# Two attention heads in the partition halves: masked keys, a shorter diagonal and 64-row value products in a four-block kernel

## The chip, the cores and the metric

One core of a Trainium2 chip runs the program. The metric is the device time of one execution in microseconds (us); the kernel before has a median of 531.84 us over three runs (530.72 to 532.0). The engines are named as in the profile: PE (TensorE matmul) with its weight loads PEld, DVE (VectorE), ACT (ScalarE), POOL (GpSimd) and SP (SyncE, which issues most DMAs).

## What is computed

The input is 2048 tokens of 512 features. Four residual blocks follow each other, A, B, A, B, with layer norm ahead of each. Both have 32 heads of 16 features. A is attention in four segments of 512 tokens, causal within the segment, plus a read from a memory that gathers the earlier segments. B is linear attention with softmax feature maps.

```python
# A, for each segment s of 512 tokens (q, k, v: head, token, 16)
logits = einsum('bhqd,bhkd->bhqk', qs, ks) * 0.25 + mask     # mask: -1e9 above the diagonal
a_dot = einsum('bhqk,bhkd->bhqd', softmax(logits), vs)
a_mem = einsum('bhld,bhde->bhle', phi(qs), M) / (einsum('bhld,bhd->bhl', phi(qs), z) + 1e-6)
out_s = g * a_mem + (1 - g) * a_dot                          # g = sigmoid(beta), per head
M += einsum('bhld,bhle->bhde', phi(ks), vs); z += sum_l phi(ks)
# B, over all 2048 tokens
phi_q = concat(softmax(q @ w_phi), softmax(-q @ w_phi))      # phi_k alike
o = phi_q @ (phi_k^T v) / (phi_q @ sum(phi_k) + 1e-6)
```

## The kernel before

The whole input lives in SBUF as 16 token tiles of 128 rows. Each operation is an entry of a graph (`Graph.op`, line 130) with its reads and writes; a table written out in the file (ORDER, line 979) gives the order of all operations, the engine of those that may run on two, and the buffer of each tile. `place` (line 156) reads it, `emit` (line 189) writes one instruction stream per engine with semaphore waits. So each engine takes its work strictly in the table's order, and nothing is rearranged when the program runs.

Block A. `a_proj` (line 610) makes one segment's operands for four groups g of eight heads: keys KT and queries QT (128 features x 512 tokens), and from QT four masked copies Q4 (line 642), each of which keeps every fourth head. Values VT are token-major, 17 columns for a head, the last of them ones, so that a product with them gives the softmax denominator too. `a_att` (line 677) handles one token tile of 128 queries, i being its place in the segment. For each group and each block j <= i of 128 keys:

- a logits product fills a two-bank PSUM buffer S (pool pD, two buffers): two matmuls, one for each 64-row half hf of the features, with 128 keys as weights and four masked query copies (512 columns) moving. The result is 128 keys x 8 heads x 128 queries;
- ACT takes the exponential of 1024 columns into a tile PT of SBUF (line 701 calls the helper at 329);
- on the diagonal, j = i, POOL zeroes what lies above it with two affine selects of 512 columns (line 705);
- PE multiplies: for each head PT's 128 keys x 128 queries are the weights and VT's 17 columns move, written two or three times over by the access pattern of `pvitem` (line 670), so 34 or 51 columns. Sums run over j in a value bank PV of PSUM (pool pG; two such banks).

One bank PV holds two groups (line 688). Behind its two groups come, from segment 1 on, small products for the memory's denominator in the same bank (line 719, eight columns, and an epsilon row), a reciprocal (line 723, helper 367) and a multiply (line 725), both on DVE; meanwhile the other bank takes the next two groups. Then the memory read (line 731), the transpose of the result by a DMA on SP, and the output projection (line 738) with the residual.

Block B. `b_keys` (line 812) and `b_query` (line 848) share the engines: key blocks of B are interleaved with A's later tiles, B's queries follow after the last segment, since they need all keys. All matmuls are issued by the helper at line 323, most exponentials by 329, PSUM copies by 337 (ACT) and 338 (DVE).

A warm-up (line 591) keeps PE running while the first loads land. It holds some matmuls on the 64-row form, pairs in which one works on feature rows 0 to 63 and the other on rows 64 to 127.

Of the kernel before, what the change touches and what calls it, by code (L numbers as in the profile page):

```python
# [9 lines left out]
ACT = mybir.ActivationFunctionType  # L10
# [6 lines left out]
D = 512  # L17
H = 32
# [276 lines left out]
class Kernel:  # L295
# [78 lines left out]
    def alloc(self):  # L374
# [8 lines left out]
        self.eps8 = sb("eps8", [128, 8], BF16)  # L383
# [37 lines left out]
        self.pools = [self.pK, self.pX, self.pQ, self.pV, self.p1, self.p2, self.pT, self.pS, self.pD, self.pG]  # L421
# [5 lines left out]
    def setup(self):  # L427
# [38 lines left out]
        for g in range(NG):  # L466
# [34 lines left out]
        for i, tv in enumerate(self.pV.tensors):  # L501
            self.pV.init[i] = v(lambda e, tv=tv: e.memset(tv[:, :, :, 16:17], 1.0), 560, [], [], eng=P, label="one")
        v(lambda e: e.tensor_copy(self.Rz1[:, :, :, 1], self.H8[:, None, :].to_broadcast([128, 8, 8])), 130,
# [87 lines left out]
    def warm(self):  # L591
# [12 lines left out]
        for k in range(N_WARM):  # L604
            unit(128, 512, 1)
            if k == N_WARM // 2:
                for rows, n, m, c0 in ((64, 51, 12, 0), (64, 17, 8, 64), (64, 51, 8, 0), (64, 128, 8, 0), (128, 34, 8, 0), (128, 34, 8, 64), (128, 34, 8, 0)):
                    unit(rows, n, m, c0)

    def a_proj(self, L, s):  # L610
# [3 lines left out]
        st["KT"], st["Q4"], st["PhQ"], st["PhK"] = [], [], [], []  # L614
        VT = st["VT"] = self.T(self.pV, "VT")
        first = (L, s) in MASKED
        for g in range(NG):
# [3 lines left out]
            KT = self.T(self.pK, "KT")  # L621
# [3 lines left out]
            st["KT"].append(KT)  # L625
# [10 lines left out]
            QT = self.T(self.p1, "QT")  # L636
            Q4 = self.T(self.pQ, "Q4")
# [3 lines left out]
            for sl in range(4):  # L641
                fn = lambda e, Q4=Q4, QT=QT, sl=sl: e.tensor_scalar(Q4.t[:, sl, :], QT.t[:], self.m4[:, sl:sl + 1], None, op0=ALU.mult)  # L642
                self.g.op({"dve": (262.0, fn)}, [QT, R("m4")], [Q4[sl]], label="Qm", port=True)
            st["Q4"].append(Q4)
# [3 lines left out]
        for tt in range(4):  # L648
            ps = self.T(self.pG, "gen")
            self.vproj(ps, self.WA["v"], [R("WAv", i) for i in range(4)], tt, xT, opens=[VT], label="V")  # L650
            self.evac(lambda tt=tt: VT.t[:, tt, :, 0:16], lambda ps=ps: ps.t[:, 0:512].rearrange("p (h d) -> p h d", h=H),
                      512, [ps[0]], [VT[tt]], label="Vev")
        if s < 3:
            for hp in range(2):
                ps = self.T(self.pG, "gen")
                gs = (hp * 2, hp * 2 + 1)
                self.mm(lambda gs=gs, ps=ps: [(ps.t[:, (g % 2) * 136:(g % 2 + 1) * 136], st["PhK"][g].t[:, tt * 128:(tt + 1) * 128],
                                               VT.t[:, tt, 8 * g:8 * g + 8, :], tt == 0, tt == 3) for g in gs for tt in range(4)],
# [10 lines left out]

    def pvitem(self, PV, c, P, V, st, sp):  # L670

        n = 3 if 2 * c >= 2 * PVW - 495 and c >= PVW - 400 and c + 2 * (PVW - c) <= 495 else 2
        a = PV.t[:, c:c + 17]
        w = int(a.ap[0][0])
        return (bass.AP(a.tensor, int(a.offset), [[w, 128], [PVW - c, n], [1, 17]]), P, V[:, None, :].to_broadcast([128, n, 17]), st, sp)

    def a_att(self, L, s, i):
        R, v = self.R, self.v
        st = self.seg[(L, s)]
        VT = st["VT"]  # L680
        t = s * 4 + i
        Rt = self.T(self.pS, "R")
        rden = lambda: Rt.t[:, 0:64].rearrange("p (h k) -> p h k", k=2)
        o = self.T(self.p1, "o")
        nk = 2 if s >= 1 else 1
        mb = s - 1
        for hp in range(2):
            PV = self.T(self.pG, "pv")
            pvv = lambda PV=PV: PV.t[:, 0:288].rearrange("p (h c) -> p h c", c=18)
            for gg in range(2):  # L690
                g = hp * 2 + gg
                KT, Q4 = st["KT"][g], st["Q4"][g]
                PTs = []
                for j in range(i + 1):
                    S = self.T(self.pD, "S")
                    PT = self.T(self.p2, "PT")
                    self.mm(lambda S=S, KT=KT, Q4=Q4, j=j: [
                        (S.t[:, hf * 512:(hf + 1) * 512], KT.t[64 * hf:64 * hf + 64, j * 128:(j + 1) * 128],
                         Q4.t[64 * hf:64 * hf + 64, :, i * 128:(i + 1) * 128], True, True) for hf in range(2)],
                        [512], [KT] + [Q4[sl] for sl in range(4)], [S], opens=[PT], label="S", rows=64)  # L700
                    self.act(lambda PT=PT: PT.t[:], lambda S=S: S.t[:], ACT.Exp, 1024, [S], [PT], scale=0.25, label="exp")
                    if j == i:
                        for hh in range(2):
                            pt4 = lambda PT=PT, hh=hh: PT.t[:, hh * 512:(hh + 1) * 512].rearrange("p (h q) -> p h q", h=4)
                            v(lambda e, pt4=pt4: e.affine_select(pt4(), pt4(), [[0, 4], [1, 128]], ALU.is_ge, 0.0, base=0, channel_multiplier=-1),  # L705
                              587, [PT], [PT[hh]], eng="pool", label="mask")
                    PTs.append(PT)

                def pvmm(PV=PV, PTs=PTs, g=g, gg=gg):
                    r = []  # L710
                    for hl in range(8):
                        c = (gg * 8 + hl) * 18
                        for j in range(i + 1):
                            r.append(self.pvitem(PV, c, PTs[j].t[:, hl * 128:(hl + 1) * 128], VT.t[:, j, 8 * g + hl, :], j == 0, j == i))
                    return r
                self.mm(pvmm, [17] * (8 * (i + 1)), PTs + [PTs[i][0], PTs[i][1]] + [VT[j] for j in range(i + 1)], [PV[gg]], label="PV")
                if s >= 1:
                    PQ = st["PhQ"][g]
                    self.mm(lambda PV=PV, PQ=PQ, g=g, gg=gg, pvv=pvv: [
                        (pvv()[:, gg * 8:gg * 8 + 8, 17], PQ.t[:, i * 128:(i + 1) * 128], self.MSb[mb][:, g, :, 16], True, False),  # L720
                        (pvv()[:, gg * 8:gg * 8 + 8, 17], self.onesb[:], self.eps8[:], False, True)],
                        [8, 8], [PQ, PV[gg], R("MSb", mb, hp), R("onesb"), R("eps8")], [PV[("d", gg)]], label="NMd")
            v(lambda e, pvv=pvv, hp=hp: self.recip(e, rden()[:, hp * 16:hp * 16 + 16, 0:nk], pvv()[:, :, 16:16 + nk]), self.dur_recip(16 * nk),
              [PV[0], PV[1]] + ([PV[("d", 0)], PV[("d", 1)]] if s >= 1 else []), [Rt[hp]], label="rden")
            v(lambda e, pvv=pvv, hp=hp: e.tensor_tensor(o.t[:, hp * 256:(hp + 1) * 256].rearrange("p (h d) -> p h d", h=16), pvv()[:, :, 0:16],  # L725
                                                        rden()[:, hp * 16:hp * 16 + 16, 0:1].to_broadcast([128, 16, 16]), ALU.mult), 340,
              [PV[0], PV[1], Rt[hp]], [o[hp]], label="pvn")
        if s >= 1:
            NM = self.T(self.pG, "nz")
            tmp = self.T(self.p1, "nmt")  # L730
            self.mm(lambda: [(NM.t[:, g * 128:(g + 1) * 128], st["PhQ"][g].t[:, i * 128:(i + 1) * 128], self.MSb[mb][:, g, :, 0:16], True, True)
                             for g in range(NG)], [128] * 4, list(st["PhQ"]) + [R("MSb", mb, 0), R("MSb", mb, 1)], [NM], opens=[tmp], label="NM")
            v(lambda e: e.tensor_tensor(tmp.t[:].rearrange("p (h d) -> p h d", h=H), NM.t[:, :].rearrange("p (h d) -> p h d", h=H),
                                        rden()[:, :, 1:2].to_broadcast([128, H, DH]), ALU.mult), 602, [NM, Rt[0], Rt[1]], [tmp], label="nmn")
# [175 lines left out]
    def build(self):  # L910
# [9 lines left out]
        for L in range(2):  # L920
            if L == 0:
                lnA(0, 0)
                gate = self.xnop[3]
                for o in self.loads[self.early:self.second] + list(self.pV.init.values()):
                    o.deps.add(gate)
# [38 lines left out]
N_XT, N_Q4, N_K1, N_K2, N_VT, N_SM, N_KT = 5, 6, 22, 19, 5, 6, 6  # L964
PVW = 288
CAP1 = {"KT": 8, "QT": 4, "phiQ": 8, "PhK": 4, "E": 8, "xn": 3, "phe": 3, "phiKT": 2}
CAP2 = {"EQ": 16, "ET": 6}
# [12 lines left out]
c-rlEW0)<=vTa6M?e1mUwr$(CZQHhO+qP}nHg8t<+Iz3Han8H<y<hj8n%|r`D>E`MB4T7!G!z996dlDt;ZZ>p6(LjzML-f2Mu3W-qNo_cC?YD3!l6h=p%N  # L980
$wq9`&diAo`cN~2t;3=*g;Du<Gyn24kDr~=B3Dxx$f52}RnqRJ>4iiPr_<fsZti&CJ>NTd8HF-nK3qV&k1*r)(XgtDMbs2Z{;E2@sNp&BRy%8qKHj3_0_f
ij^~C?~3gQlr|a4yubfpcbej>V&$XmZ%HrjJl#$s2^&L;-Ky*E3`rV(HN8f#Y5R3A)1Baqp_$5ii_%@*{D7mgqET4Xdar2mY@M>Ihup+q8zXQEk)VkB3gt
7qlM@ax`)Q02`DEFL=DhlG!ZpKx!^jwjP9dG=nBdWjnQe;1U*1a(GAoLok8<abMz2hMUPNh)DyKsz0gfG1ocMk(KU1n^+9LRZ8Q{3LO!T3I){d#JE$NGN0
ZTcv;vJlg&;3nK*eAsN(*^l6`F#kB41P-Mxttv52hhMR2W8~bl{JwLrN$C`5^#>$3<W?ssX{M0MvyLR1;pIk`Mt$#X%?{j*TPXKvWM1yhgPl71W1lxE5?f
# [109 lines left out]
```

## Time and profile before

| | |
|---|---|
| median of three runs | 531.84 us |
| the profiled execution | 537.12 us, its span 535.1 us |
| mean granted TensorE clock | 0.990 |
| exponentials of 1024 columns | 384, mean 1041 ns (320 of the attention) |
| masks on POOL | 256, busy 164.0 us |
| mask multiplies on DVE (line 642) | 128, mean 389 ns |
| logits matmuls, 64 rows | 640, mean 387 ns |
| value matmuls, 34 or 51 columns | 2560, a mean of 179 or 187 ns |

How to read the profile: the busy time of an engine is the union of its instructions. A matmul's own time includes its way through the array, so matmuls that follow each other closely overlap in the list, and the distance of their starts tells what one of them costs. A line of the groups gives line, engine, operation, out<-in, the shapes with their count, then busy us and mean ns of one, then the idle time ahead of them with what ended it. A line of the waits names who waited for whom, the total in us, how often, and the longest. "issue" stands where nothing that the profile shows was waited for. The form "64*128" of a matmul says that it uses 64 rows and 128 columns of the array.

### The profile page before, as it was taken

To read this page: it belongs to the slowest core of one execution; us is meant where nothing else is said; L and a number is where in the kernel's file an instruction comes from. 1 tells how busy PE (TensorE), PEld (TensorE's weight loads), DVE (VectorE), ACT (ScalarE), POOL (GpSimd) and SP (SyncE) were. 2 spreads that over 40 slices of the span, in tenths; PEclk is the share of its full clock that TensorE was granted. 3 is DMA by queue.
4 is the path that set the end of the run, shared out by engine and by line. 5 is a ranking of instruction groups with operands and counts; after the bars stand their busy time and mean duration, and the time that the engine had idled before them with its cause. 6 is when DMAs were issued, how large, how long until landed. Compare 5 with 4: busy or idle time off the path is not lost.

```text
span 535.1 us, 13744 instructions
## 1 busy us (share of the span) xinstructions
PE 491.3 (92%) x5587; PEld 260.3 (49%) x5664; DVE 459.3 (86%) x1083; ACT 474.7 (89%) x616; POOL 220.9 (41%) x392
## 2 busy tenths in 40 slices
PE   9887799999999999999998879998999999999886
PEld 4333345354555455556643444453544555455653
DVE  5989999997977989778999989986988988867865
ACT  4688999999999989877997999997999999988964
POOL 4468356435645442201350753643184375320000
PEclk9999999999999999998999999998999999999989
DMA  8099332211121110000343241131111211100245
GB/s 236 19 234 137 59 70 32 50 22 30 32 41 22 21 35 17 11 2 1 61 78 70 50 80 27 24 52 22 31 21 31 31 22 31 31 13 1 50 110 137
DMA packets 84990, 27.39 MB, mean 51 GB/s; under 512 B 75680, under 2 KB 84928, under 8 KB 84928
## 3 DMA queue, kind: packets, MB, share of 16 engines
q1 hardware_dynamic: 84864, 26.50, 25.6%
q8 instruction: 44, 0.72, 0.6%
q14 instruction: 18, 0.15, 0.1%
q0 software_dynamic: 64, 0.02, 0.1%
HBM read 6.32 MB, written 2.10 MB: 16 GB/s over the span
## 4 chain that ended last, share of the span: by engine, by line
PE 46%; DVE 28%; ACT 17%; DMA 5%; issue 2%; POOL 1%; SPq 0%
PE G L323 29%; ACT p L329 16%; PE D L323 14%; DVE pQ L642 4%; DMA p<-p 4%; DVE stats L538 3%; DVE p L588 2%; PE D L601 2%; DVE pS L826 2%; DVE p L586 1%; DVE p L587 1%; DVE p L900 1%; DVE X L765 1%; DVE p L338 1%; DVE p L725 1%
## 5 line engine op out<-in xcount | busy, mean ns | idle before, releaser
L329 ACT ACTIVATE p<-D 128x1024 bf16<-128x1024 f32 x384 | 376.1, 1041 | 27.7 <-PE D L323 24.2
L705 POOL TENSOR_SCALAR_AFFINE_SELECT p<-p 128x512 bf16<-128x512 bf16 x256 | 164.0, 665 | 154.4 <-ACT p L329 153.7
L323 PE MATMUL D<-pQ,pK 64*128 64x512 bf16 x640 | 117.5, 387 | 5.6 <-ACT p L329 4.2
L323 PE MATMUL G<-pV,p 128*128 128x51 bf16 (+2 forms) x2656 | 93.5, 186 | 3.4 <-DVE p L725 2.1
L323 PEld LDWEIGHTS G<-pV,p 128*128 128x128 bf16 x2656 | 80.8, 96 | 29.7 <-issue 16.9
L329 ACT ACTIVATE p<-G 128x512 bf16<-128x512 f32 x112 | 67.6, 618 | 5.2 <-PE G L323 3.5
L323 PEld LDWEIGHTS D<-pQ,pK 64*128 64x128 bf16 x640 | 29.5, 93 | 75.2 <-ACT p L329 32.8
L546 POOL TENSOR_SCALAR rstd<-mv 128x1 f32<-128x1 f32 x60 | 17.0, 285 | 99.3 <-DVE mv L539 97.4
L826 DVE TENSOR_REDUCE pS<-p 128x32 f32<-128x512 bf16 x64 | 42.4, 675 | 13.8 <-ACT p L329 13.7
L642 DVE TENSOR_SCALAR pQ<-p,m 128x512 bf16<-128x512 bf16 x128 | 44.1, 389 | 3.5 <-ACT p L337 2.2
L538 DVE BATCH_NORM_STATS2 stats<-X 128x6 f32<-128x512 bf16 x64 | 43.3, 683 | 2.7 <-DMA X<-in_A_x_dram 1.6
L765 DVE TENSOR_TENSOR X<-X,G 128x512 bf16<-128x512 bf16 x48 | 32.4, 676 | 11.8 <-PE G L323 10.8
L808 DVE TENSOR_TENSOR pT<-G,pT 128x1024 bf16<-128x1024 f32 x30 | 36.5, 1215 | 4.8 <-PE G L323 4.3
L548 POOL TENSOR_TENSOR rstd<-rstd,mhalf 128x1 f32<-128x1 f32 x60 | 36.5, 612 | 3.5
L323 PE MATMUL G<-WA_o,p 128*128 128x512 bf16 x117 | 30.6, 380 | 4.6 <-DMA p<-p 2.2
L323 PE MATMUL G<-WB_k,pX 128*128 128x512 bf16 x119 | 31.2, 386 | 3.8 <-DMA pX<-p 2.6
L323 PE MATMUL G<-WB_o,p 128*128 128x512 bf16 x123 | 33.2, 394 | 1.0 <-DMA p<-p 0.4
L323 PE MATMUL G<-WA_v,pX 128*128 128x512 bf16 x120 | 30.5, 380 | 3.4 <-DVE p L725 1.7
L323 PE MATMUL G<-pX,WA_q 128*128 128x512 bf16 x118 | 30.1, 380 | 3.6 <-DVE mv L539 2.0
L323 PE MATMUL G<-WB_v,pX 128*128 128x512 bf16 x115 | 30.7, 382 | 1.8 <-issue 0.7
L323 PE MATMUL G<-pX,WA_k 128*128 128x512 bf16 x118 | 30.3, 380 | 1.2 <-issue 0.8
L323 PE MATMUL D<-pX,WB_q 128*128 128x512 bf16 x120 | 29.6, 379 | 0.5
(103 smaller groups left out, 669.9 us busy)
## 6 DMA issues: line engine op xcount, KB each, us to landing
out_dram<-X SPq DMA_DIRECT2D x16, 128.0 KB, 1.8
X<-in_A_x_dram SPq DMA_DIRECT2D x3, 512.0 KB, 6.2
pX<-in_B_wqkv_dram SPq DMA_DIRECT2D x3, 512.0 KB, 5.3
p<-p SPq DMA_TRANSPOSE x76, 2.5
pX<-p SPq DMA_TRANSPOSE x54, 2.5
X<-in_A_x_dram SPq DMA_DIRECT2D x4, 128.0 KB, 2.2
WA_k<-in_A_wk_dram SPq DMA_DIRECT2D x2, 256.0 KB, 4.8
WA_q<-in_A_wq_dram SPq DMA_DIRECT2D x2, 256.0 KB, 4.9
```

The lines of the kernel that those rows point to most:

```text
L323: ins = e.matmul(out_ap, lhsT, rhs, start=st, stop=sp, tile_position=(basep(lhsT), basep(out_ap)))
L329: return self.g.op({"act": (dur, lambda e: e.activation(out_ap(), in_ap(), func, scale=scale))}, reads, writes, opens, label=label)
L538: v(lambda e: e.bn_stats(self.stats[:, t, :], self.X[:, t, :]), 602, [R("X", t)], [R("st", t)], label="bn")
L546: v(lambda e: e.tensor_scalar(rs, self.mv[:, t, 1:2], LN_EPS, None, op0=ALU.add), 170, [R("mv", t)], [R("rstd", t)], eng="pool", label="rstd")
L548: v(lambda e: e.tensor_tensor(rs, rs, self.mhalf[:], ALU.pow), 540, [R("rstd", t), R("mhalf")], [R("rstd", t)], eng="pool", label="rstd")
L588: v(lambda e: e.tensor_tensor(dst.t[:], dst.t[:], e_.t[:], ALU.add), 335, [dst, e_], [dst], label="phadd", port=True)
L601: ins = e.matmul(D.t[c0:, r0 * 8:r0 * 8 + n], r[:, c0:], ones(r, n), start=True, stop=True, tile_position=(r0, c0))
L642: fn = lambda e, Q4=Q4, QT=QT, sl=sl: e.tensor_scalar(Q4.t[:, sl, :], QT.t[:], self.m4[:, sl:sl + 1], None, op0=ALU.mult)
L705: v(lambda e, pt4=pt4: e.affine_select(pt4(), pt4(), [[0, 4], [1, 128]], ALU.is_ge, 0.0, base=0, channel_multiplier=-1), 587, [PT], [PT[hh ...
L765: self.v(lambda e: e.tensor_tensor(self.X[:, t, :], self.X[:, t, :], ps.t[:, 0:512], ALU.add), 602, [R("X", t), ps[0]], [R("X", t)], label ...
L808: v(lambda e: e.tensor_tensor(dst(), ps.t[:, None, 0:512].to_broadcast([128, 2, 512]).rearrange("p s (g d h) -> p s g d h", g=NG, h=8), rz ...
L826: fn = lambda e, sgn=sgn, E=E, Z=Z: e.tensor_reduce(Z.t[:, sgn * 32:(sgn + 1) * 32], E.t[:, sgn * 512:(sgn + 1) * 512].rearrange("p (h d) ...
```

## The change

The mask moves from the queries to the keys. `a_proj` now makes KM from KT: for each half hf of the features, each of two head pairs p and each half x of a key block, a weight of 64 rows x 128 columns, whose columns 0 to 63 are 64 keys for one head and columns 64 to 127 the same keys for another. The count of multiplies stays at four per group and segment. A logits product then puts one head in partitions 0 to 63 and another in 64 to 127, and takes eight matmuls of 128 moving columns (two halves hf x two pairs x two key halves) in place of two of 512.

On the diagonal the second half of the keys needs only the second half of the queries, so a block has 192 columns for a pair of key halves, 768 in all. The triangle is added by a product: two more matmuls (weights `two64`, moving `tri`, 256 columns) add -1e9 where a query precedes its key. The POOL masks are not issued (PMASK has every tile). The exponentials of a diagonal block go to new tiles (pool pE, four buffers), whose first 64 columns are zeroed once at the start.

The value products take 64 rows each: 16 of them for a group and a key block, alternately on partitions 0 to 63 into one bank and on 64 to 127 into the other. Where the key half does not stand in the right partitions, they read VS, a copy of half of the values with the partition halves swapped, which two DMAs on SP make for each segment. Both value banks stay open over all four groups of a token tile; then each is normalized. The memory's denominators are one product of an epsilon row and four of eight columns for the whole tile, with a reciprocal of their own.

Buffers: p1 22 to 20, p2 19 to 18, the cap of B's exponentials 16 to 12. The warm-up has other shapes. The order table is new as a whole.

```diff
+            KM = self.T(self.pQ, "KM")
+            for sl in range(4):
+                fn = lambda e, KM=KM, KT=KT, sl=sl: e.tensor_scalar(
+                    KM.t[:, :, sl % 2, :, 64 * (sl // 2):64 * (sl // 2) + 64], KT.t[:].rearrange("p (j h k) -> p j h k", j=4, h=2),
+                    self.m4[:, sl:sl + 1], None, op0=ALU.mult)
-            for sl in range(4):
-                fn = lambda e, Q4=Q4, QT=QT, sl=sl: e.tensor_scalar(Q4.t[:, sl, :], QT.t[:], self.m4[:, sl:sl + 1], None, op0=ALU.mult)
...
+        for z in range(VSP):
+            t0, t1 = z * 4 // VSP, (z + 1) * 4 // VSP
+            for hf in range(2):
+                a = lambda hf=hf, t0=t0, t1=t1: VS.t[64 * hf:64 * hf + 64, t0:t1]
+                b = lambda hf=hf, t0=t0, t1=t1: VT.t[64 - 64 * hf:128 - 64 * hf, t0:t1, 16 * hf:16 * hf + 16, :]
+                self.g.op({"sp": (650.0, lambda e, a=a, b=b: [e.dma_start(a(), b())])}, [VT[i] for i in range(t0, t1)], [VS[(z, hf)]],
+                          kind="d", lat=1900.0, label="vsw", ndma=1)
...
-        n = 3 if 2 * c >= 2 * PVW - 495 and c >= PVW - 400 and c + 2 * (PVW - c) <= 495 else 2
-        return (bass.AP(a.tensor, int(a.offset), [[w, 128], [PVW - c, n], [1, 17]]), P, V[:, None, :].to_broadcast([128, n, 17]), st, sp)
+        k = int(V.ap[0][1])
+        return (bass.AP(a.tensor, int(a.offset), [[w, 128], [PVW - c, 2], [1, 17]]), P, V[:, None, :].to_broadcast([k, 2, 17]), st, sp)
...
+                    for p in range(2):
+                        for x in range(2):
+                            for hf in range(2):
+                                c = hf * 512 + (p * 192 + 64 * (1 - x) if dg else p * 256 + x * 128)
+                                c0 = 64 if dg and x else 0
+                                r.append((S.t[:, c:c + 128 - c0], k(hf, p, x), q(hf, c0), not (dg and pem) or p + x == 0, not (dg and pem)))
+                    if dg and pem:
+                        for hf in range(2):
+                            r.append((S.t[:, hf * 512:hf * 512 + 384].rearrange("p (a b) -> p a b", a=2)[:, :, 0:128], self.two64[64 * hf:64 * hf + 64].rearrange("p a b -> p (a b)"),
+                                      self.tri[64 * hf:64 * hf + 64, None, :].to_broadcast([64, 4, 64]), False, True))
...
+                    self.act(lambda PT=PT: PT.t[:, :, 64:256], lambda S=S: S.t[:, :].rearrange("p (a b) -> p a b", a=2)[:, :, 0:384].rearrange("p a (c e) -> p a c e", c=2),
+                             ACT.Exp, 768, [S], [PT], scale=0.25, label="expd")
...
+            def pvmm(PTs=PTs, g=g):
+                r = []
+                for hf in range(2):
+                    for p in range(2):
+                        k = 4 * g + 2 * hf + p
+                        for j in range(i + 1):
+                            for x in range(2):
+                                for ab in range(2):
+                                    if j == i:
+                                        P = PTs[j].t[64 * ab:64 * ab + 64, hf * 2 + p, 128 * (1 - x):128 * (2 - x)]
+                                    else:
+                                        c = hf * 512 + p * 256 + x * 128
+                                        P = PTs[j].t[64 * ab:64 * ab + 64, c:c + 128]
+                                    V = VT.t[64 * ab:64 * ab + 64, j, 16 * ab + k, :] if x == ab else VS.t[64 * ab:64 * ab + 64, j, k, :]
+                                    r.append(self.pvitem(PV[ab], 18 * k, P, V, j == 0 and x == 0, j == i and x == 1))
+                return r
...
+            self.mm(lambda: [(mc(), self.onesb[:], self.eps32[:], True, False)] +
+                    [(PV[0].t[:, 288 + 8 * g:296 + 8 * g], PQ[g].t[:, i * 128:(i + 1) * 128], self.MSb[mb][:, g, :, 16], False, g == NG - 1) for g in range(NG)],
+                    [32] + [8] * 4, list(PQ) + [R("MSb", mb, 0), R("MSb", mb, 1), R("onesb"), R("eps8")], [PV[0]["d"]], label="NMd")
...
-N_XT, N_Q4, N_K1, N_K2, N_VT, N_SM, N_KT = 5, 6, 22, 19, 5, 6, 6
-PVW = 288
+N_XT, N_KM, N_K1, N_K2, N_VT, N_SM, N_QT, N_PE = 5, 6, 20, 18, 5, 6, 6, 4
+PVW = 320
+VSP = 1
+PMASK = {(L, t) for L in range(2) for t in range(16)}
```

More of the change, by code (lines that the diff above doesn't have):

```diff
@@ L502, in setup @@
             self.pV.init[i] = v(lambda e, tv=tv: e.memset(tv[:, :, :, 16:17], 1.0), 560, [], [], eng=P, label="one")
+        for i, tp in enumerate(self.pE.tensors):
+            self.pE.init[i] = v(lambda e, tp=tp: e.memset(tp[:, :, 0:64], 0.0), 330, [], [], eng=P, label="one")
         v(lambda e: e.tensor_copy(self.Rz1[:, :, :, 1], self.H8[:, None, :].to_broadcast([128, 8, 8])), 130,
@@ L606, in warm @@
             if k == N_WARM // 2:
-                for rows, n, m, c0 in ((64, 51, 12, 0), (64, 17, 8, 64), (64, 51, 8, 0), (64, 128, 8, 0), (128, 34, 8, 0), (128, 34, 8, 64), (128, 34, 8, 0)):
-                    unit(rows, n, m, c0)
+                for rows, n, m in ((64, 51, 12), (64, 64, 8), (64, 256, 4), (128, 34, 8)):
+                    unit(rows, n, m)
     def a_proj(self, L, s):
@@ L649, in a_proj @@
             ps = self.T(self.pG, "gen")
-            self.vproj(ps, self.WA["v"], [R("WAv", i) for i in range(4)], tt, xT, opens=[VT], label="V")
+            self.mm(lambda tt=tt, ps=ps: [(ps.t[:, 0:512], xT.t[:, dt, tt * 128:(tt + 1) * 128],
+                                           self.WA["v"][:, dt, :].rearrange("p (k a e) -> p a k e", k=8, a=2), dt == 0, dt == 3) for dt in range(4)],
+                    [512] * 4, [xT[tt]] + [R("WAv", i) for i in range(4)], [ps[0]], opens=[VT], label="V")
             self.evac(lambda tt=tt: VT.t[:, tt, :, 0:16], lambda ps=ps: ps.t[:, 0:512].rearrange("p (h d) -> p h d", h=H),
                       512, [ps[0]], [VT[tt]], label="Vev")
+        for z in range(VSP):
[5 more added lines that the diff above has]
+                          kind="d", lat=1900.0, label="vsw", ndma=1)
         if s < 3:
@@ L656, in a_proj @@
                 gs = (hp * 2, hp * 2 + 1)
-                self.mm(lambda gs=gs, ps=ps: [(ps.t[:, (g % 2) * 136:(g % 2 + 1) * 136], st["PhK"][g].t[:, tt * 128:(tt + 1) * 128],
-                                               VT.t[:, tt, 8 * g:8 * g + 8, :], tt == 0, tt == 3) for g in gs for tt in range(4)],
+                self.mm(lambda gs=gs, ps=ps: [
+                    (ps.t[:, (g % 2) * 136:(g % 2 + 1) * 136].rearrange("p (k a e) -> p a k e", k=2, a=2), st["PhK"][g].t[:, tt * 128:(tt + 1) * 128],
+                     VT.t[:, tt].rearrange("p (a k r) c -> p a k (r c)", a=2, r=2)[:, :, 2 * g:2 * g + 2, :], tt == 0, tt == 3) for g in gs for tt in range(4)],
                         [136] * 8, [st["PhK"][g] for g in gs] + [VT[i] for i in range(4)], [ps[0]], label="M")
@@ L679, in a_att @@
         st = self.seg[(L, s)]
-        VT = st["VT"]
+        VT, VS = st["VT"], st["VS"]
         t = s * 4 + i
         Rt = self.T(self.pS, "R")
-        rden = lambda: Rt.t[:, 0:64].rearrange("p (h k) -> p h k", k=2)
+        rden = lambda: Rt.t[:, 0:32]
+        rmem = lambda: Rt.t[:, 32:64]
         o = self.T(self.p1, "o")
-        nk = 2 if s >= 1 else 1
         mb = s - 1
[L687 to L700, printed above, removed]
-                    self.act(lambda PT=PT: PT.t[:], lambda S=S: S.t[:], ACT.Exp, 1024, [S], [PT], scale=0.25, label="exp")
[L702 to L712, printed above, removed]
-                        for j in range(i + 1):
[L714 to L727, printed above, removed]
@@ new lines, in a_att @@
+        if s >= 1:
+            PQ = st["PhQ"]
+            mc = lambda: PV[0].t[:, 288:320]
+            self.mm(lambda: [(mc(), self.onesb[:], self.eps32[:], True, False)] +
+                    [(PV[0].t[:, 288 + 8 * g:296 + 8 * g], PQ[g].t[:, i * 128:(i + 1) * 128], self.MSb[mb][:, g, :, 16], False, g == NG - 1) for g in range(NG)],
+                    [32] + [8] * 4, list(PQ) + [R("MSb", mb, 0), R("MSb", mb, 1), R("onesb"), R("eps8")], [PV[0]["d"]], label="NMd")
+        for ab in range(2):
+            pvv = lambda ab=ab: PV[ab].t[:, 0:288].rearrange("p (h c) -> p h c", c=18)
+            rd = lambda ab=ab: rden().rearrange("p (k a r) -> p k a r", a=2, r=2)[:, :, ab, :]
+            v(lambda e, pvv=pvv, rd=rd: self.recip(e, rd(), pvv()[:, :, 16].rearrange("p (k r) -> p k r", r=2)), self.dur_recip(16),
+              [PV[ab][g] for g in range(NG)] + ([PV[ab]["d"]] if s >= 1 and ab == 0 else []), [Rt[ab]], label="rden")
+            v(lambda e, pvv=pvv, rd=rd, ab=ab: e.tensor_tensor(
+                o.t[:].rearrange("p (k a r d) -> p k a r d", a=2, r=2, d=16)[:, :, ab], pvv()[:, :, 0:16].rearrange("p (k r) d -> p k r d", r=2),
+                rd()[:, :, :, None].to_broadcast([128, 8, 2, 16]), ALU.mult), 340,
+              [PV[ab][g] for g in range(NG)] + ([PV[ab]["d"]] if s >= 1 and ab == 0 else []) + [Rt[ab]], [o[ab]], label="pvn")
@@ L729, in a_att @@
+        if s >= 1:
+            v(lambda e: self.recip(e, rmem(), mc()), self.dur_recip(32), [PV[0]["d"]], [Rt[2]], label="rden")
             NM = self.T(self.pG, "nz")
@@ L923, in build @@
                 gate = self.xnop[3]
-                for o in self.loads[self.early:self.second] + list(self.pV.init.values()):
+                for o in self.loads[self.early:self.second] + list(self.pV.init.values()) + list(self.pE.init.values()):
                     o.deps.add(gate)
```

215 lines of the change are left out of this document (123 added, 92 removed).

## The prediction, made blind

> **What bounds the kernel now.** I read the page first, then the work by stage, the waits, the groups by form, and the order of matmuls on PE in the middle of a layer.
>
> ```profile
> span 535.1 us, 13744 instructions
> PE 491.3 (92%) x5587; PEld 260.3 (49%) x5664; DVE 459.3 (86%) x1083; ACT 474.7 (89%) x616; POOL 220.9 (41%) x392
> PE 46%; DVE 28%; ACT 17%; DMA 5%; issue 2%; POOL 1%; SPq 0%
> ```
>
> Three engines are nearly full, and the chain that ended last runs over all three; POOL, whose mask is removed, holds 1% of it. So the question is which engine sets the pace in each stage. The columns below are PE, weight loads, DVE, ACT and POOL, busy us of 20:
>
> ```profile
> 40.00:60.00 20.00, 15.72 (x196) 7.53 (x198) 19.90 (x52) 18.47 (x23) 14.58 (x28) 1.00 0.87 120
> 140.00:160.00 20.00, 19.54 (x302) 11.43 (x303) 16.83 (x42) 18.93 (x22) 9.46 (x18) 1.00 0.22 41
> 440.00:460.00 20.00, 19.29 (x255) 10.39 (x256) 17.37 (x36) 19.57 (x25) 10.75 (x20) 1.00 0.18 34
> 500.00:520.00 20.00, 17.43 (x202) 11.74 (x202) 15.63 (x37) 14.77 (x24) 0.00 (x0) 0.91 0.44 100
> ```
>
> Early in layer 0 DVE is full (19.90). In the attention proper (140:160, 440:460) PE and ACT are both within about 5% of full, and a saving on one alone soon meets the other. The last stage, and the query stage between the layers, hold no attention, and the change does nothing there. Who waits for whom (us in total, times, longest):
>
> ```profile
> POOL p L705 <- ACT p L329: 153.7, 83, 5.7
> PEld G L323 <- issue: 50.8, 203, 0.8
> PEld D L323 <- ACT p L329: 35.9, 82, 1.0
> PE D L323 <- ACT p L329: 6.0, 16, 0.8
> PEld G L323 <- POOL p L705: 4.7, 15, 0.7
> PE G L323 <- POOL p L705: 0.7, 2, 0.3
> PEld G L323 <- DVE p L725: 4.2, 10, 1.6
> PE G L323 <- DVE p L725: 3.8, 4, 1.1
> ```
>
> PE waits 35.9 + 6.0 = 41.9 us for exponentials to free a logits buffer (D), only 4.7 + 0.7 = 5.4 us for masks, and 4.2 + 3.8 = 8.0 us for the normalization that frees a value bank. The 50.8 us with no partner come next.
>
> **Mode changes, the largest term.** In order of time on PE (start, us):
>
> ```profile
> 139.99 1.02 PE L323 MATMUL G<-WA_o,p 128*128 128x512 bf16 x4
> ...
> 141.79 0.39 PE L323 MATMUL D<-pQ,pK 64*128 64x512 bf16 x2
> 142.11 0.58 PE L323 MATMUL G<-pV,p 128*128 128x34 bf16 x16
> 142.63 0.39 PE L323 MATMUL D<-pQ,pK 64*128 64x512 bf16 x2
> ```
>
> Four 512-column products take 1.02 us of which the last one's own 0.38 us is latency: (1.02 - 0.38)/3 = 0.213 us each. The two 64-row logits products run side by side, so they too should free PE after 0.213 us; the value product starts 0.32 us after them, 0.10 us late. The last of its 16 starts at about 142.11 + 0.58 - 0.18 = 142.51 and the next would be due 0.026 us later, yet the logits start at 142.63, again 0.10 us late. So a change between the 64-row and the 128-row form costs 0.10 us. Logits products are these:
>
> ```profile
> L323 PE MATMUL D<-pQ,pK x640: 372/386/631, 14.5 to 474.8; 64*128 64x512 bf16 x160
> ```
>
> 640 products, first and last start 14.5 and 474.8 us, in pairs. Counting, in the trace's matmuls by order of start, each change of form: 520, or 52 us. The change gives the value products the 64-row form too. In the present order, with value products counted as 64-row and the small denominator products (which the change gathers once per token tile) left out, 388 changes are left. The new order table is data that I don't unfold, so the count after is open: 520 if value products stay next to 128-row work (a gain of nothing), 388 by the present order, fewer if the new order puts them next to logits. I take 370, near the count by the present order: 150 x 0.10 = **-15.0 us**; bounds 0 and -25 (270 left).
>
> **Logits and diagonal.** The warm-up shows 64-row pairs, each product with its own weights:
>
> ```profile
> 6.29 0.37 PEld L601 LDWEIGHTS D<-onesb 64*128 64x128 bf16 x24 [0.42 <-issue]
> L601 PE MATMUL D<-onesb 64*128 64x128 bf16 x16 | 0.6, 217 | 0.0
> ```
>
> 24 loads (12 pairs, for 51-column products) begin within 0.37 - 0.09 = 0.28 us: 0.025 us a pair. Eight pairs of 128 columns: (0.6 - 0.217)/7 = 0.055 us a pair. An off-diagonal block becomes four such pairs: 0.220 against 0.213, x 192 = **+1.3**. A diagonal block becomes two pairs of 128 columns, two of 64 (between the rows, nearer to 51 columns: 0.030) and the triangle pair of 256 columns (half of 0.213, 0.107): 0.277 against 0.213, x 128 = **+8.2** (6 to 11 by the ends of the two unseen sizes). Both fall in stages where PE is full, so all of it counts.
>
> **Value products.**
>
> ```profile
> L323 PE MATMUL G<-pV,p 128*128 128x34 bf16 x800 | 30.5, 179 | 2.7 <-DVE p L725 2.1 <-DVE pV L338 0.4
> L323 PE MATMUL G<-eps,onesb 128*128 128x8 bf16 x96 | 15.6, 169 | 0.0
> ```
>
> Now 2560 of them at (0.58 - 0.18)/15 = 0.026 us (quoted above); after, 5120 in 2560 pairs on two row halves, 0.025 a pair by the warm-up: **0**. A rule speaks against this. The Trainium skill (TensorEngine Tiling (Array Packing), Instruction Overhead) gives each matmul about 60 cycles, one column costing what 60 do, and advises against taking a tiling factor from a dimension that is already small; 17 columns are. By that rule the extra products cost another 60 to 70 us; the warm-up row disagrees for 24 products, since there the floor is paid once per pair. The denominator products fall from 192 (96 with the epsilon row above, 96 with the memory) to 120: 72 x 0.026 = **-1.9**.
>
> **Exponentials and masks.**
>
> ```profile
> L329 ACT ACTIVATE p<-D 128x1024 bf16<-128x1024 f32 x384 | 376.1, 1041 | 27.7 <-PE D L323 24.2
> L329 ACT ACTIVATE p<-G 128x512 bf16<-128x512 f32 x112 | 67.6, 618 | 5.2 <-PE G L323 3.5 <-DVE pK L338 1.2
> L705 POOL TENSOR_SCALAR_AFFINE_SELECT p<-p 128x512 bf16<-128x512 bf16 x256 | 164.0, 665 | 154.4 <-ACT p L329 153.7
> ```
>
> (1041 - 618)/512 = 0.83 ns a column, so 256 columns less are 0.21 us, x 128 diagonals = 27 us off ACT. What reaches the end lies between the waits it shortens directly (98 waits of PE for exponentials, of which 128/320 behind a diagonal: 39 x 0.21 = 8 us) and all 27. PE is full beside it, so I take **-12**, nearer the lower. The masks' 164 us leave POOL; what PE loses to them is the 5.4 us above, and it then waits for the exponential itself: **-4** (0 to -5.4).
>
> **DVE, banks, transfers.**
>
> ```profile
> L642 DVE TENSOR_SCALAR pQ<-p,m x128: 314/344/812, 12.6 to 422.9; 128x512 bf16<-128x512 bf16 x128
> L642 DVE TENSOR_SCALAR pQ<-p,m 128x512 bf16<-128x512 bf16 x128 | 44.1, 389 | 3.5 <-ACT p L337 2.2 <-PE D L323 1.1
> L725 DVE TENSOR_TENSOR p<-G,pS 128x256 bf16<-128x256 f32 x64 | 26.4, 414 | 0.9
> L367 DVE RECIPROCAL pS<-G 128x32 f32<-128x32 f32 x48 | 16.2, 341 | 9.3 <-PE G L323 9.1
> L367 DVE RECIPROCAL pS<-G 128x16 f32<-128x16 f32 x16 | 3.9, 243 | 0.1
> X<-in_A_x_dram SPq DMA_DIRECT2D x4, 128.0 KB, 2.2
> L502 POOL MEMSET pV<- x2: 654/807/960, 6.2 to 6.5; 128x128 bf16 x2
> ```
>
> The mask multiplies move from queries to keys, same count and size. Their mean is 389 ns, the median 344 and the longest 812: counted in the trace, the 41 that run while POOL is busy average 486 ns, the other 87 343. Without the masks some 128 x 0.045 = 6 us go here and a similar amount in DVE's other short bf16 operations. Against it, 24 token tiles take two reciprocals of 16 and one of 32 for two of 32: 24 x (2 x 0.243 - 0.341) = +3.5 us; setup adds three short operations. DVE is full only early (40:60): **-1** (-6 to +4).
>
> Now a token tile's value products use two banks one after the other, and one is normalized while the other fills. After, both stay open until the fourth group, so the next tile's value products wait for two reciprocals and two multiplies, 2 x (0.243 + 0.414) = 1.3 us. Behind that wait on PE's queue stands whatever the order put next, and ACT follows when its two logits buffers are empty. Today 64 turnovers cost 8.0 us; 32 turnovers with no bank in hand could cost 32 x 1.3 = 42, or nothing where logits and projections stand ahead of them. I take twice today's: **+8**.
>
> Each of 8 segments gets two transfers that swap value halves (64 rows x 4 x 544 B = 139 KB each); the 128 KB row lands in 2.2 us. They stand in SP's queue behind the value copy, and the transposes behind them wait as well. Where a segment's projections run well ahead it is hidden; uncovered it is 8 x 2.2 = 18. I take only the first segment: **+2**. Four memsets of 256 columns on POOL (128 columns took 0.8 us, so some 6 us) fall where masks used to run: 0, or 6 if the early normalizations wait behind them.
>
> **Sum:** -15.0 + 1.3 + 8.2 - 1.9 - 12 - 4 - 1 + 8 + 2 = -14.4 us. The profiled execution itself took 537.12 us (span 535.1 and 2 us around it), 1% above the median of the runs, 531.84. So the span goes to 520.7, that execution to about 522.7, and the median to **517.4**. Its own range, by the ends of the open terms, is 505 to 528.
>
> **Rivals.**
> - *ACT sets the pace alone.* All 27 us come off, and PE's gaps close as the order lets it run ahead: 15 more, 502. For it: PE's 41.9 us of waits for exponentials. Against: PE 19.54 of 20 in 140:160. 0.15.
> - *The forms stay mixed.* If the new order keeps 128-row work between logits and value products, the 15 us stay and the diagonal is still paid: 532.4. Against: logits and value products already stand side by side above. 0.08.
> - *The banks decide.* The wait for both normalizations takes the place of the mask's. At full price 42 instead of 8: 551; it decides the sign from about 22 us, 0.7 us a tile, uncovered. For it: PE has little other work late in a layer, and 8.0 us are paid today with a bank in hand. Against: a tile's logits stand ready as cover. 0.13.
> - *Pairs don't overlap.* 2560 more products x 0.026 = 67 us, on a full PE: 584. For it: the warm-up's pairs share one set of ones and are few; a long burst must also be supplied at four instructions per 0.025 us. Against: the 0.025 itself. The skill's rule above would give this. 0.06.
>
> The forecast has 0.58. A measurement of this kernel tells apart about 0.3%, 1.6 us. Faster: the forecast, the first rival and little of the others, 0.74; within 0.3%: 0.07, nearly all from mixed forms; slower: 0.19. The range takes in ACT alone and half of the bank case: 500 to 541; it leaves out non-overlapping pairs, the full bank price and a gain past 500, together under 0.2.
>
> **What would show it.** Right: the gaps "issue" before weight loads of value products nearly gone and PE's fall from 50.8 us; exponentials of 768 columns at about 0.83 us; 64-row value products at 0.025 us a pair; POOL under 70 us busy; DVE's mask multiplies at 344 ns mean; ACT near 448 us busy. Wrong: value products twice as long on PE; waits of PE for the normalization above 22 us; PE's waits for the swap at each segment; more form changes than 450.

## The result and the profile after

The changed kernel takes 518.8 us (median of four runs, 517.68 to 520.41) against 531.56 for the kernel before (a fourth run beside the three known ahead): a ratio of 0.9764, 95% interval 0.9734 to 0.9795, 12.8 us less. The forecast was 517.4 us, 14.4 less. The profiled execution after took 518.31 us, near its median, while the one before (537.12) lay 5 us above its own; so the spans differ by 18.5 us, and the runs decide. Of two experiments below, the control with 64-row pairs and the one with both put back, one run was over 1.5% longer than the fastest of its kernel, at a lower clock, and is left out of the times and ratios.

The page, first part and chain:

```profile
span 516.6 us, 22854 instructions
PE 486.2 (94%) x10288; PEld 300.1 (58%) x10288; DVE 435.5 (84%) x1106; ACT 449.0 (87%) x620; POOL 56.8 (11%) x142
PE 64%; ACT 16%; DVE 8%; DMA 7%; issue 3%; POOL 0%; SPq 0%
```

DVE fell from 459.3 to 435.5 us, ACT from 474.7 to 449.0, and PE's share of the chain rose from 46% to 64%: PE alone now leads more often. Matmuls nearly doubled, 5664 to 10288 (the trace of before lacks 77 of its own), and PE's busy time did not grow with them. Middle of layer 1, PE in order of time (start, us; at the second mark stand the other 61 value products of this group):

```profile
427.00 0.40 PE L323 MATMUL D<-pK,pQ 64*128 64x128 bf16 x8
427.33 0.19 PE L323 MATMUL G<-eps,onesb 128*128 128x32 bf16 x1
...
427.56 0.40 PE L323 MATMUL D<-pK,pQ 64*128 64x128 bf16 x8
427.79 0.18 PE L323 MATMUL G<-pV,p 64*128 64x34 bf16 x1
427.80 0.20 PE L323 MATMUL G<-pW,p 64*128 64x34 bf16 x2
...
428.61 0.38 PE L323 MATMUL D<-pK,pQ 64*128 64x128 bf16 x8
```

From logits to a 128-row product 0.33 us pass, from logits to value products 0.23: the change of form is gone. The 64 value products from 427.79 to 428.61 take 0.82 us, 0.0256 a pair, over 32 pairs and not only the 12 of the warm-up; and the logits follow without a gap. Counted over the whole trace, 330 changes of form are left of 520. The waits; first one line of before that the prediction does not show, then those after (pW holds VS, the swapped values):

```profile
PEld D L323 <- issue: 30.1, 72, 0.8
```

```profile
PEld D L323 <- issue: 20.2, 43, 1.5
PEld D L323 <- ACT p L329: 19.1, 46, 0.9
PEld G L323 <- issue: 18.5, 35, 2.3
PEld D L323 <- ACT pE L329: 12.5, 30, 0.7
PEld G L323 <- DMA pW<-pV: 3.4, 2, 2.5
PE G L323 <- DMA pW<-pV: 2.3, 1, 2.3
PE D L323 <- ACT p L329: 2.3, 6, 0.9
PE D L323 <- ACT pE L329: 1.8, 6, 0.5
```

"issue" ahead of weight loads fell from 50.8 + 30.1 to 18.5 + 20.2 us. PE's waits for exponentials fell only from 41.9 to 35.7. New are 5.7 us for the swap. The normalization is missing from the list; in its own view nothing stands under those who waited for it:

```profile
L782 DVE TENSOR_TENSOR p<-G,pS x64: 360/415/426, 38.6 to 459.7; 128x256 bf16<-128x256 f32 x64
its engine sat idle before it (us, times) until:
who waited for it (us, times):
```

The groups, by form (count, then busy us and mean ns), and the swap's DMA (KB, us to landing):

```profile
L329 ACT ACTIVATE p<-D 128x1024 bf16<-128x1024 f32 x256 | 255.5, 1040 | 24.2 <-PE D L323 22.8
L329 ACT ACTIVATE pE<-D 128x768 bf16<-128x768 f32 x128 | 102.5, 827 | 10.4 <-PE D L323 9.3
L642 DVE TENSOR_SCALAR pQ<-p,m 128x512 bf16<-128x512 bf16 x128 | 41.1, 351 | 4.3 <-PE D L323 3.7 <-ACT p L337 0.6
L367 DVE RECIPROCAL pS<-G 128x16 f32<-128x16 f32 x64 | 13.5, 234 | 12.4 <-PE G L323 12.2
L516 POOL MEMSET pE<- 128x256 bf16 x4 | 1.4, 382 | 0.0
pW<-pV SPq DMA_DIRECT2D x16, 136.0 KB, 3.5
```

The exponential of 768 columns takes 827 ns as worked out (1040 less 0.21 us), the mask multiplies a mean of 351 ns instead of 389.

### The profile page after: what moved, and what is told of

Read it like the earlier page. It is cut to its first block, busy times and chain, and to the rows that moved or that the text cites. A ratio compares the mean times of both kernels' runs of the same rounds, so it can differ in the third digit from the quotient of the medians.

```text
span 516.6 us, 22854 instructions
## 1 busy us (share of the span) xinstructions
PE 486.2 (94%) x10288; PEld 300.1 (58%) x10288; DVE 435.5 (84%) x1106; ACT 449.0 (87%) x620; POOL 56.8 (11%) x142
## 3 DMA queue, kind: packets, MB, share of 16 engines
q1 hardware_dynamic: 89216, 28.73, 30.1%
## 4 chain that ended last, share of the span: by engine, by line
PE 64%; ACT 16%; DVE 8%; DMA 7%; issue 3%; POOL 0%; SPq 0%
PE G L323 44%; PE D L323 18%; ACT p L329 13%; DMA p<-p 6%; ACT pE L329 2%; PE D L615 2%; DMA pW<-pV 1%; DMA pX<-p 1%; DVE p L338 1%; DVE stats L552 1%; DVE p L782 1%; ACT pS L329 1%; DVE pQ L642 1%; PE G L356 1%; DVE p L959 1%
## 5 line engine op out<-in xcount | busy, mean ns | idle before, releaser
L329 ACT ACTIVATE p<-D 128x1024 bf16<-128x1024 f32 x256 | 255.5, 1040 | 24.2 <-PE D L323 22.8
L323 PE MATMUL D<-pK,pQ 64*128 64x128 bf16 (+1 forms) x2560 | 111.8, 212 | 6.4 <-issue 3.2
L329 ACT ACTIVATE pE<-D 128x768 bf16<-128x768 f32 x128 | 102.5, 827 | 10.4 <-PE D L323 9.3
L323 PEld LDWEIGHTS D<-pK,pQ 64*128 64x128 bf16 x2560 | 71.3, 94 | 55.9 <-issue 19.5
L323 PE MATMUL G<-pV,p 64*128 64x34 bf16 (+1 forms) x1632 | 76.0, 178 | 2.8 <-issue 2.8
L323 PE MATMUL G<-pV,pE 64*128 64x34 bf16 x1024 | 72.5, 175 | 3.8 <-DMA pW<-pV 2.3
L323 PEld LDWEIGHTS G<-pV,p 64*128 64x128 bf16 (+1 forms) x1632 | 69.5, 93 | 10.1 <-issue 6.6
L323 PE MATMUL G<-pW,pE 64*128 64x34 bf16 x1024 | 71.1, 175 | 0.0
L323 PE MATMUL G<-pW,p 64*128 64x34 bf16 x1536 | 67.6, 176 | 1.4 <-issue 1.2
L323 PEld LDWEIGHTS G<-pW,p 64*128 64x128 bf16 x1536 | 62.9, 93 | 1.3 <-issue 0.9
```

The costliest lines, as they stand in the source:

```text
L323: ins = e.matmul(out_ap, lhsT, rhs, start=st, stop=sp, tile_position=(basep(lhsT), basep(out_ap)))
L329: return self.g.op({"act": (dur, lambda e: e.activation(out_ap(), in_ap(), func, scale=scale))}, reads, writes, opens, label=label)
```

## The experiments

Each has a ratio to the kernel before, measured beside it on the same chip. To compare with the changed kernel I take the difference of the ratios (its own is 0.9764, from the first measurement; it was not run again beside each) times 531.6 us; every such number is uncertain by 2 to 4 us.

| | ratio | 95% | us against the changed kernel |
|---|---|---|---|
| 256 changes of form put back | 1.0122 | 1.0067 to 1.0178 | +19.0 |
| its control, 64-row pairs | 0.9822 | 0.9763 to 0.9881 | +3.1 |
| no triangle | 0.9669 | 0.9628 to 0.9710 | -5.1 |
| diagonal exponentials of 1024 | 1.0003 | 0.9971 to 1.0034 | +12.7 |
| no wait for the swap | 0.9753 | 0.9695 to 0.9811 | -0.6 |
| masks on POOL | 1.1013 | 1.0973 to 1.1053 | +66.4 |
| changes of form and 1024 columns | 1.0173 | 1.0125 to 1.0221 | +21.7 |
| longer reciprocals | 0.9796 | 0.9746 to 0.9847 | +1.7 |
| its control, longer reductions | 0.9870 | 0.9832 to 0.9908 | +5.6 |

| | ratio | 95% | us against the kernel before |
|---|---|---|---|
| small masks | 0.9883 | 0.9851 to 0.9915 | -6.2 |
| exponentials of 768 | 0.9897 | 0.9863 to 0.9931 | -5.5 |
| both | 0.9842 | 0.9806 to 0.9878 | -8.4 |

### What a change of form costs the end

```diff
                         k = 4 * g + 2 * hf + p
+                        if (hf, p) == (1, 0):
+                            r.append((PV[0].t[:, 320:354], self.onesb[:], VT.t[:, 0, 0:2, :].rearrange("p h c -> p (h c)"), True, True))
```

> The changed kernel with one product more in the middle of each of the 128 value products: 128 rows, 34 columns, into columns that nothing reads, so the form changes twice more for each, 256 changes. Theory (a change of form costs 0.10 us on PE and PE sets the pace): 256 x 0.10 + 128 x 0.026 = +29 us on the changed kernel's 518.8, about 548. Rival (PE's remaining waits absorb it): +10 at most, under 529.

The control puts a pair of 64-row products there:

```diff
+                        if (hf, p) == (1, 0):
+                            for ab in range(2):
+                                r.append((PV[ab].t[:, 320:354], self.onesb[64 * ab:64 * ab + 64, :], VT.t[64 * ab:64 * ab + 64, 0, 0:2, :].rearrange("p h c -> p (h c)"), True, True))
```

> The same with a 64-row pair in place of the 128-row product, so no change of form is added. Theory: 128 x 0.025 = +3 us, about 522. Rival (the extra instructions and their weights cost, not the form): as much as the kernel with the 128-row product.

The first took 539.26 us, the control 522.41. The page with the products of 128 rows, and their group:

```profile
PE 514.2 (95%) x10416; PEld 320.7 (59%) x10416; DVE 436.1 (81%) x1106; ACT 453.9 (84%) x620; POOL 57.2 (11%) x142
L323 PE MATMUL G<-pV,onesb 128*128 128x34 bf16 x128 | 24.4, 191 | 0.0
```

PE's busy time rises by 28.0 us for 128 products, nearly the 29 expected; DVE and POOL stay as they were. Of that, 19.0 reach the end, 3.1 with the form left alone. So the form and not the instruction costs, but a change of 0.10 us on PE is worth (19.0 - 3.1)/256 = 0.06 us at the end (0.045 to 0.08 by the uncertainties): the theory's mechanism, at 0.6 of its size.

### The triangle and the exponentials

```diff
-                    if dg and pem:
+                    if dg and pem and False:
                         for hf in range(2):
                             r.append((S.t[:, hf * 512:hf * 512 + 384]...
```

Not shown is one flag more, by which the sums now close with the logits' own last product.

> The changed kernel without the triangle's product (the causal mask inside a diagonal block is left out). Theory (the diagonal's extra time on PE is paid in full): 128 x 0.107 = -13.7 us, about 505. Rival (ACT sets the pace there, PE's product is hidden): -3 at most, over 515.

515.58 us. The triangle's 13.7 us of PE time are worth 5.1 at the end (1.5 to 9 by the intervals): between the two expectations, nearer to the rival's. PE's waits for exponentials ahead of weight loads are 19.8 and 15.3 us in this trace, together 35.1, against 31.6 with the triangle:

```profile
PEld D L323 <- ACT p L329: 19.8, 45, 0.9
PEld D L323 <- ACT pE L329: 15.3, 39, 0.8
```

So part of the time that PE saves it seems to spend waiting for ACT; but the trace is of a run above the median (519.04 us), and 3.5 us are less than half of the 8.6 that do not reach the end.

```diff
-                    self.act(lambda PT=PT: PT.t[:, :, 64:256], lambda S=S: S.t[:, :].rearrange(...)[:, :, 0:384]...,
-                             ACT.Exp, 768, [S], [PT], scale=0.25, label="expd")
+                    self.act(lambda PT=PT: PT.t[:].rearrange("p a b -> p (a b)"), lambda S=S: S.t[:, :],
+                             ACT.Exp, 1024, [S], [PT], scale=0.25, label="expd")
```

> The changed kernel with diagonal exponentials of 1024 columns again (the zeros of the new tiles are overwritten, so the sums over the diagonal are not the reference's): 27 us more on ACT, nothing else. The prediction's share: +12 us, about 531. ACT sets the pace: +27, about 546. ACT has slack: the direct waits alone, +8 or less, under 527.

531.76 us: +12.7, the prediction's share, and no more than half of what ACT does in addition. The group, and PE's waits behind it:

```profile
L329 ACT ACTIVATE pE<-D 128x1024 bf16<-128x1024 f32 x128 | 131.3, 1066 | 5.4 <-PE D L323 4.8
PEld D L323 <- ACT p L329: 25.4, 62, 0.9
PEld D L323 <- ACT pE L329: 23.5, 58, 0.7
```

131.3 against 102.5 us on ACT; PE's loads wait 48.9 us for it instead of 31.6.

### Both put back

> The changed kernel with both the 256 changes of form (alone +20 us) and the 1024-column diagonal exponentials (alone +12.8; the diagonal's sums are not the reference's). Theory (PE and ACT cover each other, whichever is later counts): clearly less than the sum, +20 to +27, 539 to 546. Rival (they lie in separate places): the sum, +33, about 552.

The edit joins that of the changes of form and that of the 1024 columns. 541.24 us, +21.7, where the single effects add up to 31.7: as the theory had it, PE and ACT cover each other, and of two delays mostly the larger one counts. With the changes of form in place the 1024 columns add only 21.7 - 19.0 = 2.7 us (uncertain by some 4), not 12.7.

### The swap

```diff
-                                    V = VT.t[64 * ab:64 * ab + 64, j, 16 * ab + k, :] if x == ab else VS.t[64 * ab:64 * ab + 64, j, k, :]
+                                    V = VT.t[64 * ab:64 * ab + 64, j, 16 * ab + k, :]
...
-            self.mm(pvmm, [], PTs + [PTs[i][0], PTs[i][1]] + [VT[j] for j in range(i + 1)] + vs, [PV[0][g], PV[1][g]], label="PV", rows=64, dur=8 * (i + 1) * 25.5)
+            self.mm(pvmm, [], PTs + [PTs[i][0], PTs[i][1]] + [VT[j] for j in range(i + 1)], [PV[0][g], PV[1][g]], label="PV", rows=64, dur=8 * (i + 1) * 25.5)
```

> The changed kernel with value products that read the unswapped values throughout (half of the sums take the wrong keys' values) and so never wait for the swap; the transfers still run. The prediction's term: -2 us, about 517. Theory from the trace of the changed kernel (PE waits 3.4 + 2.3 us for the swap, all of it on the path): -6, about 513. Rival (other work would have been late anyway): 0.

519.33 us. PE's three waits of 5.7 us are gone from the list, and the time is the same (-0.6, uncertain by 3 to 4). A saving of 5.7 is not borne out; one of 2 can't be told from none.

### Masks on POOL again

The branch that issues the selects still stands in the changed kernel, and the constant below turns it on. A further edit, not shown, puts the selects into the order right behind their exponentials, each behind POOL's instruction before it.

```diff
-PMASK = {(L, t) for L in range(2) for t in range(16)}
+PMASK = set()
```

> The changed kernel with POOL's masks in place of the triangle's product: 128 pairs of selects on 64 rows behind the diagonal exponentials, in the same order otherwise, each behind POOL's instruction before it. Theory (leaving the triangle out gained 3 us; masks on POOL lengthen DVE's short operations and delay value products): +5 or more on the changed kernel, over 523. Rival (POOL is free work): as without the triangle, about 515.5, which would beat both kernels.

586.14 us, far above both expectations. The page, the waits and the group:

```profile
PE 499.5 (86%) x10032; PEld 300.1 (51%) x10032; DVE 459.4 (79%) x1106; ACT 452.4 (77%) x620; POOL 233.4 (40%) x398
PEld G L339 <- POOL pE L763: 49.3, 42, 3.2
PE G L339 <- POOL pE L763: 41.3, 39, 3.1
L763 POOL TENSOR_SCALAR_AFFINE_SELECT pE<-pE 64x512 bf16<-64x512 bf16 x256 | 177.3, 693 | 180.6 <-ACT pE L345 163.8
```

PE waits 90.6 us for masks, against 5.4 in the kernel before with the same number of selects. POOL is not full, 233 us of 584. The waits suggest, though no run shows it, that the new order has the value products so close behind their exponentials that there is no room for two selects in between. The selects also stand behind POOL's instruction before them, which can delay them; how much of the 66 us that makes wasn't tried. PE's own work grew as well: the same 10032 products kept it busy for 499.5 us, against 480.4 without the triangle, at a mean granted clock of 0.944 against 0.983, and by the ratio of these clocks 480.4 would become 500. What lowered the clock stays open. So as far as this run tells, the order leans on the triangle's product, and the worth of that product can't be read from leaving it out.

### The two savings in the kernel before

The masks shrink to 8 columns, in the second kernel the diagonal exponentials to 768, in the third both:

```diff
-                            pt4 = lambda PT=PT, hh=hh: PT.t[:, hh * 512:(hh + 1) * 512].rearrange("p (h q) -> p h q", h=4)
+                            pt4 = lambda PT=PT, hh=hh: PT.t[:, hh * 512:hh * 512 + 8].rearrange("p (h q) -> p h q", h=4)
-                            v(lambda e, pt4=pt4: e.affine_select(pt4(), pt4(), [[0, 4], [1, 128]], ALU.is_ge, 0.0, base=0, channel_multiplier=-1),
+                            v(lambda e, pt4=pt4: e.affine_select(pt4(), pt4(), [[0, 4], [1, 2]], ALU.is_ge, 0.0, base=0, channel_multiplier=-1),
```

> The kernel before with masks of 8 columns instead of 512 (nearly all of the causal mask inside a diagonal block is left out): POOL nearly free. The prediction's terms: -4 for the waits and -1 for DVE, about 527. Rival (DVE's 12 us of lengthened operations count in full): -12 or more, under 520. Rival (POOL hides everything): 0.

526.22 us, -6.2 (-4.5 to -7.9). DVE loses 19 us, most of it in short bf16 operations that were lengthened beside the masks:

```profile
PE 497.8 (95%) x5664; PEld 259.5 (50%) x5664; DVE 440.3 (84%) x1083; ACT 472.9 (90%) x616; POOL 107.6 (21%) x392
L642 DVE TENSOR_SCALAR pQ<-p,m 128x512 bf16<-128x512 bf16 x128 | 38.5, 346 | 3.4 <-ACT p L337 2.4 <-PE D L323 0.8
```

459.3 became 440.3, the mask multiplies' mean 346 ns instead of 389.

```diff
-                    self.act(lambda PT=PT: PT.t[:], lambda S=S: S.t[:], ACT.Exp, 1024, [S], [PT], scale=0.25, label="exp")
+                    w = 384 if j == i else 512
+                    self.act(lambda PT=PT, w=w: PT.t[:].rearrange("p (a b) -> p a b", a=2)[:, :, 0:w], lambda S=S, w=w: S.t[:].rearrange("p (a b) -> p a b", a=2)[:, :, 0:w],
+                             ACT.Exp, 2 * w, [S], [PT], scale=0.25, label="exp")
...
```

> The kernel before with diagonal exponentials of 768 columns (heads 3 and 7 of each group take their neighbour's diagonal block, and masks shrink by a quarter): ACT 27 us shorter. The prediction's term: -12, about 520 (direct waits alone: -8; ACT sets the pace: -27, about 505). What the changed kernel showed when the 256 columns were put back (+12.9): the same size here, if ACT is worth as much in both.

527.38 us, -5.5 (-3.6 to -7.3). The forecast of -12 misses, and so does the size that the changed kernel showed: the same 27 us of ACT are worth 12.7 us in the new kernel and 5.5 in the old one. The likely reason is that 52 us of changes of form keep PE later in the old one; the run with both put back fits this (2.7 instead of 12.7), but no run takes the changes of form out of the old order.

> The kernel before with both the small masks and the 768-column exponentials (the mask inside a diagonal block and the diagonals of heads 3 and 7 of each group left out). Alone they gave -6.2 and -5.5 us. Theory (PE with its 52 us of changes of form is the next limit in that order, so one gain eats into the other): -9 or less gain, over 523. Rival (each has its own waits): -12, about 520. Rival (each was hidden by the other): -18 or more, under 514.

523.4 us, -8.4, where the two alone make -11.7: they eat into each other, by 3.3 us that are uncertain by about as much. By themselves, in the old order, they are two thirds of the gain of the whole change; but they leave most of the mask out and pay no triangle for it.

### The value banks

```diff
-            v(lambda e, pvv=pvv, rd=rd: self.recip(e, rd(), pvv()[:, :, 16].rearrange("p (k r) -> p k r", r=2)), self.dur_recip(16),
+            rd3 = lambda ab=ab: Rt.t[:, 0:192].rearrange("p (m c) -> p m c", m=3)[:, :, 0:32].rearrange("p m (k a r) -> p m k a r", a=2, r=2)[:, :, :, ab, :]
+            v(lambda e, pvv=pvv, rd3=rd3: self.recip(e, rd3(), pvv()[:, :, 16].rearrange("p (k r) -> p k r", r=2)[:, None].to_broadcast([128, 3, 8, 2])), self.dur_recip(16),
```

> The changed kernel with the 64 reciprocals ahead of the normalization written three times over (48 elements): 0.2 us each, 12.8 us on DVE, and both value banks come free 0.4 us later in each of 32 token tiles. The prediction's bank term (turnovers wait on PE): +8 to +13 us. Theory from the trace of the changed kernel (no matmul waits for the normalization): no more than the same work elsewhere on DVE, +5 at most.

The control lengthens 24 of B's reductions, in the same way, to 1024 columns.

> The control: the same 12.8 us on DVE in another place, 24 reductions of the keys of B twice as long (0.53 us each); the banks come free as in the changed kernel. Bank term: 5 us or more below the kernel with long reciprocals. Theory: within 3 us of it, 518 to 524.

The groups of the two kernels, one fence each:

```profile
L367 DVE RECIPROCAL pS<-G 128x48 f32<-128x48 f32 x64 | 26.1, 433 | 11.9 <-PE G L323 11.7
```

```profile
L885 DVE TENSOR_REDUCE pS<-p 128x64 f32<-128x1024 bf16 x24 | 28.9, 1208 | 2.3 <-ACT p L329 2.3
```

Each adds about 12.7 us of DVE's operations (64 x 0.2; 24 x 0.53). 521.51 and 525.41 us: the work ahead of the banks costs +1.7, the same work elsewhere +5.6. With the longer reciprocals PE does wait for the normalization, which it did not in the changed kernel:

```profile
PEld G L323 <- DVE p L783: 2.4, 8, 0.5
PE G L323 <- DVE p L783: 0.7, 3, 0.3
```

That is 3.1 us in all, and 8 us at the end are ruled out; holding both banks longer costs no more than any work on DVE.

## Why the prediction was right, point by point

The time came within 1.4 us of the forecast, but the terms of the sum did not each hold; their errors have both signs, and that the sum lands so close is in part luck.

- **Mode changes** (-15.0). The mechanism is shown: the changes fell from 520 to 330, more than the 150 assumed, and putting 256 back costs 15.9 us beyond the control. Mis-sized is the price at the end, 0.06 us instead of 0.10; the count was off the other way. 190 x 0.06 = 11 us is an estimate: the price was measured by adding changes to the new order, and no run removes them from the old one.
- **Logits and diagonal** (+1.3, +8.2, -1.9 with the denominators). On PE right. Counted in the traces from a block's first logits product to the next product of the same form, the medians are 0.234 us off the diagonal, 0.290 on it, and 0.226 for the old pair: 192 x 0.008 + 128 x 0.064 = 9.7 us, where 9.5 were predicted. "All of it counts" was wrong: of the triangle's 13.7 us, 5.1 reach the end.
- **Value products** (0). Right: 0.0256 us a pair over 32 pairs. The rival without overlap is out. The Trainium skill (TensorEngine Tiling (Array Packing), Instruction Overhead) gives each matmul an overhead of about 60 cycles, however few its columns. The trace has 0.0256 us once for two products on the two row halves, so that rule, charged to each product, does not hold here.
- **Exponentials** (-12). 12.7 in the new kernel, 5.5 in the old: not a constant of the work saved. The term was worked out from the old kernel's waits, with 8 us as its lower bound, and there the saving is below that; that 12 fits the new kernel is partly luck.
- **Masks and DVE** (-4, -1). The small masks in the kernel before gave 6.2, the two terms together 5. DVE's relief was larger than worked out, 19 us; what it is worth apart from the waits for masks wasn't tried.
- **Banks** (+8). Wrong: no matmul waits for the normalization. I took the waits of today with half the slack; the order puts enough in front of the next tile's value products. In the trace 0.2 to 67 us, in the median 2.8, pass from the end of a tile's second normalization to the next value product.
- **Swap** (+2). PE waits 5.7 us for it, and taking the waits away gave nothing measurable.

The parts, measured alone or estimated, don't add up to the whole: 11 from the forms, 5.5 to 12.7 from the exponentials, 6.2 from the masks, less some 5 for the triangle, make 18 to 25 us where 12.8 came. The two pairs tried together (21.7 of 31.7, 8.4 of 11.7) show why at least in part, the first pair clearly: PE and ACT hide a share of each other's savings. What the new order as a whole is worth, apart from the forms that it brings together, stays open, and so does what the smaller buffers and the other warm-up cost: the order can't be run with the old operations, and the run with POOL's masks shows no more than that it does not suit masks put there. Of the variants only the one without the triangle, which leaves work out, was clearly faster than the changed kernel.

## What to carry to other kernels

Look for the gaps that no wait explains: here 0.10 us at each change between 64-row and 128-row matmuls, 520 times, and giving neighbouring products the same form removed a third of them without making PE's products dearer. Where two engines are both within a few per cent of full, price a saving on one well below its length (here 0.2 to 0.6 of it reached the end), and expect two such savings to overlap. A written-out order is part of a change: masks that cost PE 5 us of waits in the old order cost it 90 in the new one, where they also stood behind POOL's other work.

## What the runs showed of the hardware

- Two 64-row value products of 34 columns, each with its own weights, take 0.0256 us together, sustained over 64 products; 128-row products of 34 columns start 0.025 us apart in the kernel before. Doubling the matmuls cost PE nothing.
- POOL's select of 512 columns took 693 ns on 64 partitions and 665 ns on 128: half the partitions save nothing.
- A swap of 136 KB between partition halves, from SBUF to SBUF, landed after 3.5 us in the median (2.5 to 5.2), against 2.2 for the load of 128 KB on which the estimate rested.
- On POOL a memset of 256 columns in four contiguous pieces took 0.38 us in the mean, one of 128 single columns 0.68: the estimate of 1.6 for the larger was four times too high.
